# A gelu behind the next pair's copy, and a weight fold in rounded products among another block's matmuls

## The chip, the core and the metric

The kernel runs on one core of a Trainium2 chip. The core has TensorE (matmuls, called PE in the profile), VectorE (DVE), ScalarE (ACT), GpSimd (POOL) and SyncE (SP, which here only issues DMAs). The time is the device time of one execution in microseconds (us).

## What is computed

```python
x = A_x                                   # 2048 x 576
xn = _layernorm(x)
q, k, v = split(xn @ wqkv)                # 32 heads of 18
phi = lambda t: jnp.where(t > 0, t + 1, jnp.exp(t)) + 1e-6
kv = einsum("bhsd,bhse->bhde", phi(k), v) # one 18 x 18 state per head
z = einsum("bhsd->bhd", phi(k))           # sums over all tokens
o = (phi(q) @ kv) / (phi(q) . z + 1e-6)
s = o @ wo
g = silu(gelu(xn @ w1 + b1) @ w2 + b2)    # 576 -> 4608 -> 576
out = x + s * g
```

## The kernel before

All values are float32 and the error must stay small, so a matmul operand is split into a rounded part (`_h`, type fp32r) and the rest (`_l`, again fp32r), and a product is the sum of three rounded matmuls: h times h, h times l, l times h. To split, ScalarE casts (`split_w`, `set_hi`) and VectorE subtracts (`set_lo`). Some small matmuls are left in plain float32.

**First stage** (tiles `t` of 128 tokens, loop at L526): layernorm, projection to k and v (`project`, L310), phi(k), and the state, which is summed over all tiles in two PSUM banks (`state`, L379). A column of ones beside v (`VB`) gives the sums z as row 126 of the same banks.

**Between the stages** (L628 to L1079): the state of the last tile is summed, its blocks on the diagonal are copied into `kvz` with a mask, and z into `sums_k` (L635). Because the state doesn't depend on the token any more, `o @ wo` is rearranged: `fold_wo` (L681) multiplies the state with `wo` once, group by group (seven heads, 126 rows, to a group; the groups are `GROUPS`), into `kw`, and `attend` (L766) later multiplies each block's normalised phi(q) with `kw`. The fold makes 12 products of 288 columns in plain float32, each into one of two PSUM buffers (`bank1`); those of the left half (`h` = 0) are copied out by ScalarE, those of the right half by VectorE. `kw` is then moved by DMAs into tiles of 128 rows and split (`split_kw`). Two matmuls with the one-hot `last_row` spread z over all 128 rows (`zb_ps`), and ScalarE copies it to `zb`.

**Second stage** (loop at L1056, `i` from 1): for each block of 128 tokens `query` (L500; the name `pq`), `phi_query` (three ScalarE steps and one on VectorE), `by_sums` (GpSimd: phi(q) times z), `normalize` (VectorE: reduce, add, reciprocal; GpSimd: the product `pbuf`), `pad` (ScalarE copies 64 columns), `transpose_p` (TensorE, name `ptp`) and, three iterations later, `attend`.

**Third stage** (loop at L1502): the feed-forward net, in 18 steps: nine chunks of 512 hidden columns for the first half of the tokens and nine for the second. A chunk is two pairs of 256 hidden columns, `Up` (L1117), and then the products with W2 (`product`, L1266, name `pm`). Products of two by two blocks are made in seven matmul groups in place of eight, with sums and differences of operands, so `Up.step` runs seven groups of seven matmuls in the order 1, 2, 6, 5, 7, 3, 4: A, B, A, E, A, E, C. A and E are written more than once in the same PSUM bank: before group 6 adds into A, ScalarE must have copied group 1's value (`m1_sb`, L1152), before group 7 adds again it must have copied group 6's (L1158), and before group 3 adds into E it must have copied group 5's (L1162). Group 4's value C gets a VectorE sum (L1170) and then a gelu on ScalarE (L1171, the activation at L1143).

In the first half the weights are prepared beside this: GpSimd makes sums of W1 and W2, ScalarE and VectorE split them, and DMAs store them for the second half. A planner calls these pieces after fixed steps of a chunk (28 a chunk: 0 to 6 behind the first pair's groups, 7 to 13 behind the second's, then 14 of products): `PW2` for the splits of W2 (`hi` at the step, `lo` one step later), `PH` for the operands made of h (`S` sums on GpSimd, `hi` and `lo` splits). All engines but SP execute in the order in which the code is written (`in_order`), and SP's queue too is in order, so what stands ahead in an engine's queue holds all that is behind it.

Of the kernel before, what the change touches and what calls it, by code (L numbers as in the profile page):

```python
# [8 lines left out]
F32 = mybir.dt.float32  # L9
# [25 lines left out]
NSTG = 6  # L35
# [9 lines left out]
def linear_attention_gated_ffn(ctx, tc, x, xT, wqkv, wo, w1, w1e, b1, w2, b2, out):  # L45
# [68 lines left out]
    x_dram = dram.tile([P, 28, 512], F32, name="x_dram")  # L114

# [14 lines left out]
    zb = wqp.tile([P, D], F32, name="zb")  # L130


    ph1 = ExitStack()
    wkvp = ph1.enter_context(tc.tile_pool(name="wkvp", bufs=1, reuse_waits="tile"))
    stw = ph1.enter_context(tc.tile_pool(name="stw", bufs=2, reuse_waits="tile"))
    w2p = ph1.enter_context(tc.tile_pool(name="w2p", bufs=2, reuse_waits="tile"))
# [6 lines left out]
    last_row = t1.tile([P, P], F32, name="last_row", bufs=1)  # L143
    sums_k = t1.tile([P, D], F32, name="sums_k", bufs=1)
# [10 lines left out]
    def make_mask():  # L155

        nc.gpsimd.memset(sums_k, 0.0)
        nc.gpsimd.memset(last_row, 0.0)
        nc.gpsimd.affine_select(
            out=last_row, in_=last_row, compare_op=ALU.not_equal, fill=1.0, base=-G,  # L160
            pattern=[[0, P]], channel_multiplier=1,
        )
# [362 lines left out]
    raw_q = {}  # L525
    for t in range(NT):  # L526
# [101 lines left out]
    nc.sync.dma_start(b1c, b1)  # L628
    query(0)
    state(*pend)  # L630
    ln = GROUPS[-1][1]
    nc.vector.copy_predicated(kvz[:G, : 4 * G], mask[:G, :], ps_kv[0][:G, : 4 * G])
    nc.vector.copy_predicated(kvz[:ln, 4 * G : D], mask[:ln, :ln], ps_kv[1][:ln, :ln])
    nc.vector.copy_predicated(kvz[:ln, D:], mask[:ln, 8:ln], ps_kv[1][:ln, 8:ln])
    nc.scalar.copy(sums_k[96 : G + 1, : 4 * G], ps_kv[0][96 : G + 1, : 4 * G])  # L635
    nc.scalar.copy(sums_k[96 : G + 1, 4 * G :], ps_kv[1][96 : G + 1, :ln])
    query(1)
    zb_ps = bank2("zb_ps")
    for h in range(2):
        nc.tensor.matmul(  # L640
            zb_ps[:, h, :HD], last_row[: G + 1], sums_k[: G + 1, h * HD : (h + 1) * HD],
            start=True, stop=True,
        )
    ph1.close()
# [18 lines left out]
    ph2 = ExitStack()  # L663
    kwp = ph2.enter_context(tc.tile_pool(name="kwp", bufs=1, reuse_waits="tile"))
    t2 = ph2.enter_context(tc.tile_pool(name="t2", bufs=2, side="right", reuse_waits="tile"))
    wo_sb = []
    for i, (g, n) in enumerate(GROUPS):
        wo_sb.append(stage(D, f"wo{i}"))
        nc.sync.dma_start(wo_sb[i][:n], wo[g : g + n, :])
# [11 lines left out]
    def fold_wo():  # L681
# [7 lines left out]
        for i, n, at in [(i, G, i * G) for i in range(4)] + [(4, 8, 4 * G), (4, P, 512)]:  # L689
            rows = GROUPS[i][1]  # L690
            for h in range(2):
                hs = slice(h * HD, (h + 1) * HD)
                ps = bank1(f"ps_kw{i}{n}{h}")[:n, :HD]
                nc.tensor.matmul(  # L694
                    ps, kvz[:rows, at : at + n], wo_sb[i][:rows, hs], start=True, stop=True
                )
                if n < P:
                    if h:
                        nc.vector.tensor_copy(kw[i][:n, hs], ps)
# [15 lines left out]
            yield  # L715
# [340 lines left out]
    for i in range(1, NT + 4):  # L1056
        if 1 < i < NT:
            query(i)
# [3 lines left out]
        if i == 1:  # L1062
            phi_query(0)
            nc.scalar.copy(as2(zb), zb_ps[:, :, :HD])
            by_sums(0)
            groups, made = fold_wo(), []
            next(groups)
            steps = phi_steps(t2, pq.pop(1), "q1", made)
            next(steps)
            next(groups)  # L1070
            next(steps)
            next(groups)
            next(steps, None)
            phi_q[1] = made
            next(groups), next(groups)
            normalize(0)
            for _ in groups:
                pass
            pad(0)  # L1079
# [37 lines left out]
    class Up:  # L1117

# [26 lines left out]

        def step(self, i):
# [3 lines left out]
            if i == 1:  # L1150
                self.mm(A, 1)
                nc.scalar.copy(m1_sb, A)  # L1152
            elif i == 2:
# [14 lines left out]
            elif i == 4:  # L1168
                self.mm(C, 4)
                tt(C, C, u2_sb, op=ADD)  # L1170
                self.gelu(0, 1, C)  # L1171
# [279 lines left out]
    def plan_w1(add, w, base, T, hi, lo):  # L1451
# [16 lines left out]
    PW2 = {2: 0, 1: 1, 7: 3, 4: 6, 6: 7, 3: 9}  # L1468
    W2_NEXT = {1: 15, 2: 17, 7: 19, 4: 21, 5: 23, 3: 25, 6: 27}
    PH = dict(  # L1470
        S={(7, 0): 7, (5, 0): 8, (6, 0): 11, (3, 0): 11, (7, 1): 13, (5, 1): 14, (6, 1): 15, (3, 1): 15},
# [175 lines left out]
```

## Time and profile before

| | us |
|---|---|
| median of three runs (1110.47 to 1110.54) | 1110.5 |
| the profiled execution | 1110.38 |
| its span, first to last instruction | 1108.7 |
| TensorE busy | 1092.9 |
| VectorE busy | 788.5 |
| ScalarE busy | 545.5 |
| GpSimd busy | 453.1 |

In the rows shown below a timeline row gives the start, the time from the first start to the last end of the instructions merged in the row, the engine, the line, the operation with output and inputs, the shape and the count; the bracket at its end gives the idle time of the engine before it and what ended that. In the waits a row gives who waited for whom, the sum in us, the number of times and the longest. `a`, `bc` and `e` are the PSUM tiles of A, of B and C, and of E; `mid` holds the three copies, `g` the outputs of gelu.

### The profile page before, as it was taken

Reading aid. Unit: us, or ns where it says so; the run is one execution under the profiler, and the core shown is the slowest. Engines: PE = TensorE matmul, PEld = TensorE weight load, DVE = VectorE, ACT = ScalarE, POOL = GpSimd, SP = SyncE. Lnnn points to the kernel's source line nnn. Section 1 sums busy time; section 2 is a strip of 40 time slices with the busy share of each in tenths; the row PEclk is TensorE's granted clock in tenths of the full one; section 3 lists DMA queues with packets and bytes.
Section 4 is the critical chain, followed back from the end, with each engine's and each line's share of the span. In section 5 each row is a group of like instructions: output and inputs, shape, how many; then the busy total and the mean of one; then the engine's idle time right before and its main releaser. Section 6 shows DMA issues by size and latency. Waiting matters only on the chain.

```text
span 1108.7 us, 18087 instructions
## 1 busy us (share of the span) xinstructions
PE 1092.9 (99%) x6702; PEld 1007.6 (91%) x6702; DVE 788.5 (71%) x1096; ACT 545.5 (49%) x952; POOL 453.1 (41%) x394
## 2 busy tenths in 40 slices
PE   9999999999999999999999999999999999999998
PEld 8999989999898988989889889798898998989988
DVE  7766448888688887888878888565474564754756
ACT  6454555464646456464564645525244243353452
POOL 3555314332546445464454644325233233241340
PEclk9999999999999999999999999999999999999999
DMA  7997534675958559486584859977767667766452
GB/s 235 238 235 211 191 116 157 209 246 185 348 197 310 210 189 325 159 307 218 184 326 160 303 183 391 385 267 271 222 221 228 215 225 226 233 218 208 141 187 86
DMA packets 86960, 253.99 MB, mean 229 GB/s; under 512 B 11734, under 2 KB 24022, under 8 KB 84184
## 3 DMA queue, kind: packets, MB, share of 16 engines
q1 hardware_dynamic: 86872, 252.83, 68.0%
q8 instruction: 53, 0.87, 0.3%
q14 instruction: 35, 0.29, 0.1%
HBM read 156.27 MB, written 94.58 MB: 226 GB/s over the span
## 4 chain that ended last, share of the span: by engine, by line
PE 91%; DVE 3%; ACT 2%; issue 2%; DMA 2%; POOL 0%; SPq 0%; DVEq 0%; ACTq 0%; POOLq 0%
PE pm L1279 35%; PE a L1135 13%; PE e L1135 8%; PE bc L1135 8%; PE pk L321 6%; PE pq L321 5%; PE ps_s L775 5%; PE pv L321 4%; PE pd L1395 2%; DMA op<-w 2%; PE ps_kva L382 1%; PE ptp L757 1%; PE ps_kw L694 1%; DVE e L1174 1%; DVE bc L1170 1%
## 5 line engine op out<-in xcount | busy, mean ns | idle before, releaser
L1285 DVE TENSOR_TENSOR macc<-pm,macc 128x576 f32<-128x576 f32 x218 | 164.2, 753 | 53.5 <-PE pm L1279 52.4
L799 ACT CAST h_h<-g 128x512 fp32r<-128x512 f32 x204 | 122.6, 620 | 135.5 <-PE pm L1279 135.0
L802 DVE TENSOR_TENSOR h_l<-g,h_h 128x512 fp32r<-128x512 f32 x204 | 157.8, 777 | 15.7 <-ACT h_h L799 15.3
L1245 POOL TENSOR_TENSOR mid<-g 128x512 f32<-128x512 f32 x34 | 43.8, 1288 | 127.3 <-ACT g L1143 127.3
L1152 ACT COPY mid<-a 128x512 f32<-128x512 f32 x36 | 21.1, 587 | 95.2 <-PE a L1135 93.9
L1239 POOL TENSOR_TENSOR g<-g 128x512 f32<-128x512 f32 x34 | 52.2, 1536 | 35.8 <-ACT h_h L799 28.9
L1165 DVE TENSOR_TENSOR z<-a,mid 128x512 f32<-128x512 f32 x36 | 25.1, 698 | 51.8 <-PE a L1135 47.7
L845 POOL TENSOR_TENSOR w1raw<-w1raw 128x256 f32<-128x256 f32 x18 | 13.3, 738 | 116.8 <-ACT h_h L799 68.2
L1143 ACT ACTIVATE g<-bc,b1c 128x512 f32<-128x512 f32 x72 | 49.8, 691 | 18.1 <-DVE bc L1170 18.0
L1242 POOL TENSOR_TENSOR g<-g 128x512 f32<-128x512 f32 x34 | 52.6, 1547 | 10.7 <-DVE h_l L802 8.6
L1367 POOL TENSOR_TENSOR fin1l<-fin1h,fin1l 128x288 f32<-128x288 f32 x8 | 6.5, 808 | 120.9 <-DMA fin1l<-s_dram 73.0
L1155 DVE TENSOR_TENSOR bc<-bc,mid 128x512 f32<-128x512 f32 x36 | 25.0, 694 | 41.6 <-PE bc L1135 40.2
L1236 POOL TENSOR_TENSOR g<-g 128x512 f32<-128x512 f32 x34 | 47.6, 1399 | 2.7
L1158 ACT COPY mid<-a 128x512 f32<-128x512 f32 x36 | 21.1, 585 | 54.7 <-PE a L1135 54.7
L740 POOL TENSOR_TENSOR pbuf<-phiq,den 128x576 f32<-128x576 f32 x16 | 19.4, 1212 | 63.6 <-DVE den L739 63.6
L1166 ACT COPY mid<-a 128x512 f32<-128x512 f32 x36 | 21.1, 587 | 41.0 <-DVE z L1165 41.0
L321 PE MATMUL pk<-wkv_h,xh 128*128 128x288 f32 (+1 forms) x160 | 38.2, 321 | 0.5 <-DVE xh L251 0.5
L321 PE MATMUL pk<-wkv_l,xh 128*128 128x288 f32 (+1 forms) x160 | 38.2, 321 | 0.0
L775 PE MATMUL ps_s<-kw_h,th 128*128 128x288 f32 x160 | 35.5, 303 | 0.0
L802 DVE TENSOR_TENSOR h_l<-mid,h_h 128x512 fp32r<-128x512 f32 x34 | 34.1, 1004 | 1.9 <-ACT h_h L799 1.9
L1135 PE MATMUL a<-s,w 128*128 128x512 f32 x108 | 28.6, 400 | 6.4 <-ACT mid L1152 6.4
L321 PE MATMUL pq<-wq_h,xh 128*128 128x288 f32 x160 | 34.8, 299 | 0.0
(881 smaller groups left out, 3679.2 us busy)
## 6 DMA issues: line engine op xcount, KB each, us to landing
we<-we_dram SPq DMA_DIRECT2D x36, 448.0 KB
w2raw<-w SPq DMA_DIRECT2D x10, 1152.0 KB
w1raw<-w SPq DMA_DIRECT2D x18, 512.0 KB
op_a<-wa SPq DMA_DIRECT2D x18, 512.0 KB
op_c<-wc SPq DMA_DIRECT2D x18, 512.0 KB
op_d<-wd SPq DMA_DIRECT2D x18, 512.0 KB
wc<-op_c SPq DMA_DIRECT2D x18, 512.0 KB
wa<-op_a SPq DMA_DIRECT2D x18, 512.0 KB
```

The lines of the kernel that those rows point to most:

```text
L321: nc.tensor.matmul(ps[:, h, : ws.stop - ws.start], st, w[:, k, ws], start=(begin and i == 0), stop=(end and i == len(seq) - 1), skip_group ...
L775: nc.tensor.matmul(ps[:, h, :HD], st[:, k, :], w[:, k, h * HD : (h + 1) * HD], start=(i == 0), stop=(i == len(seq) - 1),)
L799: nc.scalar.copy(pair[0], src)
L802: eng.tensor_tensor(pair[1], src, pair[0].bitcast(F32), op=SUB)
L1135: nc.tensor.matmul(ps, st, mv, start=first and n == 0, stop=n == len(seq) - 1, skip_group_check=True,)
L1143: nc.scalar.activation(g, ps, AF.Gelu_apprx_tanh, bias=b1c[:, f : f + 1])
L1236: tt(src[5, pr], A(1, 0), A(1, 1), op=ADD)
L1239: tt(src[6, pr], src[5, pr], A(0, 0), op=SUB)
L1242: tt(src[3, pr], A(0, 1), src[6, pr], op=SUB)
L1245: tt(src[7, pr], A(0, 0), A(1, 0), op=SUB)
L1279: nc.tensor.matmul(ps[:, q, :HD], hs[p][st][:, cs], m[:, p, :], start=(n == 0 and i not in CHAIN), stop=(n == 5), skip_group_check=True,)
L1285: nc.vector.tensor_tensor(dst, src, dst, op=ADD)
```

## The change

It has five parts.

**The gelu of C** of the first pair of each chunk (even pair number `p`) isn't issued at the end of its pair, but in step 1 of the next pair, behind that step's copy of A. That of the second pair is issued where it was.

**Two entries of `PW2`**: W2's operand 4 is split at step 7 instead of 6, operand 6 at 8 instead of 7. **Two entries of `PH`'s sums**: (6, 1) at step 17 instead of 15, (3, 1) at 18 instead of 15.

**The fold** is made of rounded products: `wo` is split by ScalarE and VectorE behind the first query, and `kvz` behind its masked copies, and each of the 12 products becomes three rounded matmuls. The fold's generator now yields after each product. The third query is no longer made as a whole behind the fold: its 14 parts (two matmuls each) are written alternately with the products, one product behind each part from the third on. The three steps of the second query's phi are called at parts 4, 6 and 8, and the first query's `normalize` at part 10; a product's copy is written behind the part that follows it.

**z** isn't spread by matmuls any more: row 126 of `sums_k` (now the same memory as `zb`) is stored to DRAM and loaded back onto all rows. **`wo`** is loaded behind tile 14's work instead of behind the second query, and the pool `stg` has seven buffers instead of six. The pools of the first stage are closed in two steps, so that buffers of the third stage can hold the split `wo`.

```diff
-NSTG = 6
+NSTG = 7
...
+        if t == NT - 2:
+            for i, (g, n) in enumerate(GROUPS):
+                wo_sb.append(stage(D, f"wo{i}"))
+                nc.sync.dma_start(wo_sb[i][:n], wo[g : g + n, :])
...
     query(0)
+    for i in range(5):
+        split_wo(i)
+    for i in range(3):
+        wo_lo(i)
     state(*pend)
...
-    query(1)
-    zb_ps = bank2("zb_ps")
-    for h in range(2):
-        nc.tensor.matmul(
-            zb_ps[:, h, :HD], last_row[: G + 1], sums_k[: G + 1, h * HD : (h + 1) * HD],
-            start=True, stop=True,
-        )
+    nc.sync.dma_start(z_dram, sums_k[G : G + 1])
+    nc.sync.dma_start(
+        zb, bass.AP(tensor=z_dram.tensor, offset=z_dram.offset, ap=[[0, P], [1, D]])
+    )
...
+    nc.scalar.copy(kv_h[:G], kvz[:G])
+    for i in range(3, 5):
+        wo_lo(i)
+    nc.vector.tensor_tensor(kv_l[:G], kvz[:G], kv_h[:G].bitcast(F32), op=SUB)
+    query(1)
...
-                nc.tensor.matmul(
-                    ps, kvz[:rows, at : at + n], wo_sb[i][:rows, hs], start=True, stop=True
-                )
+                w = slice(at, at + n)
+                for k, (st, mv) in enumerate(((kv_h, 0), (kv_h, 1), (kv_l, 0))):
+                    nc.tensor.matmul(
+                        ps, st[:rows, w], wo_sb[i][mv][:rows, hs], start=k == 0, stop=k == 2
+                    )
+                yield
...
             phi_query(0)
-            nc.scalar.copy(as2(zb), zb_ps[:, :, :HD])
             by_sums(0)
             groups, made = fold_wo(), []
...
+            for k in range(n):
+                project(
+                    2, wq_h, wq_l, pq[2], PARTS[k : k + 1], begin=k == 0, end=k == n - 1
+                )
+                if k in (4, 6, 8):
+                    if k == 4:
+                        steps = phi_steps(t2, pq.pop(1), "q1", made)
+                    next(steps, None)
+                if k == 10:
+                    normalize(0)
+                if k > 1:
+                    next(groups)
...
+        def last(self):
+            C, f = self.bc[:, 1, :], 2 * self.p
+            self.g[0, 1] = g = gg.tile([P, 512], F32, tag="g", name="g")
+
+            def run():
+                nc.scalar.activation(g, C, AF.Gelu_apprx_tanh, bias=b1c[:, f : f + 1])
+
+            if self.p % 2:
+                run()
+            else:
+                Up.late.append(run)
...
                 nc.scalar.copy(m1_sb, A)
+                for late in Up.late:
+                    late()
+                Up.late.clear()
...
                 tt(C, C, u2_sb, op=ADD)
-                self.gelu(0, 1, C)
+                self.last()
...
-    PW2 = {2: 0, 1: 1, 7: 3, 4: 6, 6: 7, 3: 9}
+    PW2 = {2: 0, 1: 1, 7: 3, 4: 7, 6: 8, 3: 9}
```

How the rows stand on the engines: ScalarE in the second chunk of the first half, at the border of its two pairs (`bc2` and `e2` are the first pair's, `a3` the second's; `w2_1_` are splits of W2, `h10` of h). Before:

```order
L1143 ACTIVATE g_3884<-e2_3784,b1c_78 128x512
L1143 ACTIVATE g_3897<-bc2_3785,b1c_78 128x512
L799 CAST w2_1__3899<-w2raw1_3680 128x576
L1152 COPY mid_3293<-a3_3901 128x512
L799 CAST w2_1__3916<-w2raw1_3680 128x576
L799 CAST h10_h_3921<-g_3830 128x512
L1158 COPY mid_3293<-a3_3901 128x512
```

and now:

```order
L1176 ACTIVATE g_3921<-e2_3821,b1c_78 128x512
L1197 COPY mid_3330<-a3_3935 128x512
L1184 ACTIVATE g_3934<-bc2_3822,b1c_78 128x512
L828 CAST w2_1__3948<-w2raw1_3717 128x576
L828 CAST h10_h_3953<-g_3867 128x512
L828 CAST w2_1__3967<-w2raw1_3717 128x576
L1206 COPY mid_3330<-a3_3935 128x512
```

The first copy of A has moved ahead of the gelu of C and of one cast of W2; the same three casts stand between it and the next copy of A, and the gelu beside them.

GpSimd's rows stand in the same order before and now: the sums (6, 1) and (3, 1) follow the sum (5, 1) of the same pair and precede the next chunk's sums of weights, with nothing of GpSimd's written between the old and the new steps.

VectorE around the fold (`kw01` to `kw4` are the copies of the products' right halves, `phiq1` is phi of the second query, `den0` belongs to the first query's `normalize`). Before:

```order
L699 COPY kw01_1728<-ps_kw11261_1742 126x288
L699 COPY kw23_1729<-ps_kw21261_1753 126x288
L340 SCALAR_TENSOR_TENSOR phiq1_1761<-pq1_1648,eq1_1737 128x576
L699 COPY kw23_1729<-ps_kw31261_1766 126x288
L699 COPY kw4_1730<-ps_kw481_1776 8x288
L735 TENSOR_REDUCE den0_1780<-eq0_1720 128x32
L738 TENSOR_SCALAR den0_1780<-den0_1780 128x32
L739 RECIPROCAL den0_1780<-den0_1780 128x32
```

and now:

```order
L729 COPY kw01_1748<-ps_kw11261_1774 126x288
L334 SCALAR_TENSOR_TENSOR phiq1_1800<-pq1_1694,eq1_1764 128x576
L729 COPY kw23_1749<-ps_kw21261_1793 126x288
L764 TENSOR_REDUCE den0_1820<-eq0_1734 128x32
L767 TENSOR_SCALAR den0_1820<-den0_1820 128x32
L768 RECIPROCAL den0_1820<-den0_1820 128x32
L729 COPY kw23_1749<-ps_kw31261_1814 126x288
L729 COPY kw4_1750<-ps_kw481_1837 8x288
```

The copy of the sixth product (number 5, counted from 0) now stands behind phi of the second query, and that of the eighth (number 7) behind the first query's reduce, add and reciprocal.

More of the change, by code (lines that the diff above doesn't have):

```diff
@@ L114, in linear_attention_gated_ffn @@
     x_dram = dram.tile([P, 28, 512], F32, name="x_dram")
+    z_dram = dram.tile([1, D], F32, name="z_dram")
     rr_dram = dram.tile([2, P, 512], F32, name="rr_dram")
@@ L130, in linear_attention_gated_ffn @@
     zb = wqp.tile([P, D], F32, name="zb")
[L133 to L136, printed above, removed]
+    sums_k = zb
+    ph1, ph1w = ExitStack(), ExitStack()
+    wkvp = ph1w.enter_context(tc.tile_pool(name="wkvp", bufs=1, reuse_waits="tile"))
+    stw = ph1w.enter_context(tc.tile_pool(name="stw", bufs=2, reuse_waits="tile"))
+    w2p = ph1w.enter_context(tc.tile_pool(name="w2p", bufs=2, reuse_waits="tile"))
     t1 = ph1.enter_context(tc.tile_pool(name="t1", bufs=2, side="right", reuse_waits="tile"))
@@ L141, in linear_attention_gated_ffn @@
     nc.gpsimd.memset(tiny, 1e-6)
-    last_row = t1.tile([P, P], F32, name="last_row", bufs=1)
-    sums_k = t1.tile([P, D], F32, name="sums_k", bufs=1)
     v_bufs = [t1.tile([P, NG, P], F32, name=f"vb{i}", bufs=1) for i in range(2)]
@@ L155, in make_mask @@
     def make_mask():
[L157 to L161, printed above, removed]
-        )
         nc.gpsimd.memset(mf, 1.0)
@@ L627, in linear_attention_gated_ffn @@
         pend = (t, k_t, v_t)
[L628 to L636, printed above, removed]
-    query(1)
-    zb_ps = bank2("zb_ps")
-    for h in range(2):
-        nc.tensor.matmul(
-            zb_ps[:, h, :HD], last_row[: G + 1], sums_k[: G + 1, h * HD : (h + 1) * HD],
-            start=True, stop=True,
-        )
-    ph1.close()
+    ph1w.close()
     w1r = ctx.enter_context(tc.tile_pool(name="w1r", bufs=2, reuse_waits="tile"))
@@ L1117, in linear_attention_gated_ffn @@
     class Up:
+        late = []
         def __init__(self, n, w, xs):
```

56 lines of the change are left out of this document (38 added, 18 removed).

## The prediction

> **What bounds the kernel now.** I read the page first (busy time of each engine), then the waits of TensorE, then the timeline at the waits and at the place where the fold stands.
>
> ```profile
> PE 1092.9 (99%) x6702; PEld 1007.6 (91%) x6702; DVE 788.5 (71%) x1096; ACT 545.5 (49%) x952; POOL 453.1 (41%) x394
> ```
>
> ```profile
> PE a L1135 <- ACT mid L1152: 6.4, 9, 0.8
> ```
>
> The first line is the page's, the second the longest of TensorE's waits (us in total, times, longest). TensorE is busy for 1092.9 of 1108.7 us, so only two things shorten this kernel: matmul time taken away, or a wait of TensorE taken away. Busy time hides short waits, since the ends of matmuls are modelled; so I measure by the starts of matmuls. The waits name one repeated place: nine times TensorE waits before writing `a` a second time until ScalarE's copy of `a` (L1152) is done. Here is one of the nine, in the second of a chunk's two pairs (the first half of the program has nine chunks): B starts, then A again, then E, then A, then E.
>
> ```profile
> 387.41 0.39 PE L1135 MATMUL bc<-xh,wa 128*128 128x512 f32 x1
> ...
> 389.93 1.65 PE L1135 MATMUL a<-s,w 128*128 128x512 f32 x6 [0.76 <-ACT mid L1152]
> ...
> 391.65 1.53 PE L1135 MATMUL e<-s,wd 128*128 128x512 f32 x6
> ...
> 394.83 1.54 PE L1135 MATMUL e<-s,wc 128*128 128x512 f32 x6
> ```
>
> The same two blocks in a chunk of the second half, where nothing waits, and in the very first chunk:
>
> ```profile
> 755.93 0.39 PE L1135 MATMUL bc<-h0r,wa 128*128 128x512 f32 x1
> ...
> 759.10 1.07 PE L1135 MATMUL e<-s1r,wd 128*128 128x512 f32 x4
> ```
>
> ```profile
> 295.78 0.39 PE L1135 MATMUL bc<-xh,wa 128*128 128x512 f32 x1
> ...
> 299.58 0.62 PE L1135 MATMUL e<-s,wd 128*128 128x512 f32 x2
> ```
>
> B plus A take 3.17 us undisturbed (755.93 to 759.10), 4.24 where they wait (387.41 to 391.65) and 3.80 in the first chunk. The wait therefore costs 1.07 us eight times and 0.63 once, more than the 0.76 shown as idle, because the matmul pipeline is refilled behind it.
>
> **The gelu behind the copy.** ScalarE's row of work at that place:
>
> ```profile
> 388.14 0.69 ACT L1143 ACTIVATE g<-bc,b1c 128x512 f32<-128x512 f32 x1 [0.51 <-DVE bc L1170]
> 388.72 0.66 ACT L799 CAST w__4386<-w2raw 128x576 fp32r<-128x576 f32 x1
> 389.28 0.59 ACT L1152 COPY mid<-a 128x512 f32<-128x512 f32 x1
> ...
> 390.33 0.63 ACT L799 CAST h_h<-g 128x512 fp32r<-128x512 f32 x1
> ...
> 391.85 0.59 ACT L1158 COPY mid<-a 128x512 f32<-128x512 f32 x1 [0.88 <-PE a L1135]
> ...
> 394.00 0.60 ACT L1162 COPY mid<-e 128x512 f32<-128x512 f32 x1
> ```
>
> ```profile
> 387.42 0.68 DVE L1170 TENSOR_TENSOR bc<-bc,mid 128x512 f32<-128x512 f32 x1
> ```
>
> The copy of `a` stands behind the previous pair's last gelu, which waits for VectorE's sum (387.42 to 388.10), and behind a cast of W2. Its input was complete when B began (387.41) plus some 0.2 us. With the copy first it runs from about 387.6 to 388.2, and A can start when B ends, at 387.41 + 1.59 = 389.00 instead of 389.93.
>
> What the copy jumped stays on time: the gelu still waits for the same sum and starts at 388.14, and the cast of W2 follows at 388.72. So GpSimd's difference of h, which waits for that gelu, starts when it did. Next are the cast of h (389.28, 0.63) and the next cast of W2 (389.91, 0.66), done at 390.57. The next copy of `a` (L1158) now becomes due at about 390.8: it began 1.92 behind its A block, of which 0.13 was refill. It is therefore not held. From that copy to the copy of `e` (L1162) the queue is unchanged and takes 2.15 us (391.85 to 394.00), so the copy of `e` runs from 392.95 to 393.55. The E block that overwrites its source comes 3.18 behind the E before it (391.65 to 394.83), at 389.00 + 1.59 + 3.18 = 393.77. It came at 394.83 with the copy done at 394.60: the margin was 0.23 and stays 0.22. Late next is this copy, but just not late enough. I count no new wait there: the gain is 8 x 1.07 + 0.63 = 9.2 us, and I take 9.0, because a margin of 0.2 will not hold in every chunk. The bounds are 9.2 and, if the margin is missed by 0.5 in each of nine chunks, 4.5.
>
> In the second half's nine chunks the gelu is also moved behind the copy, and there TensorE did not wait before; there are no casts of W1 and W2 there, so I count nothing.
>
> **The two sums on GpSimd** are written two and three steps later, but GpSimd executes its instructions in written order, and in that order they have the same neighbours before and after: nothing moves, 0 us. The stores of two W2 operands go past one load of `we` on SP's queue; TensorE reads that load a chunk later, so this too is 0.
>
> **The fold.** TensorE's rows: the two `zb` matmuls, the fold, the third query, its transposes; then the transposes of the third block.
>
> ```profile
> 153.18 1.13 PE L640 MATMUL zb_ps<-sums_k,last_row 127*128 127x288 f32 x4
> 154.15 7.53 PE L694 MATMUL ps_kw<-wo,kvz 126*126 126x288 f32 x24
> 161.30 0.64 PE L321 MATMUL pq<-wq_h,xh 128*128 128x288 f32 x2
> ...
> 162.04 0.43 PE L321 MATMUL pq<-wq_h,xl 128*128 128x288 f32 x2
> ...
> 165.24 0.71 PE L757 MATMUL ptp<-ident,pbuf 128*128 128x128 f32 x5
> ...
> 174.00 0.71 PE L757 MATMUL ptp<-ident,pbuf 128*128 128x128 f32 x5
> ```
>
> From 162.04 to 165.24 stand twelve pairs of rounded matmuls of 288 columns: 0.267 a pair, 0.133 each. The new stretch from 153.18 on holds 14 such pairs (3.73) and 12 products of three (36 x 0.133 = 4.80): 8.53 us, where 12.06 stood (153.18 to 165.24). If nothing waited, TensorE would be at the transposes 3.5 us sooner, at 161.7. It will wait, for three reasons, each from these rows:
>
> ```profile
> 157.66 0.78 ACT L338 ACTIVATE eq<-eq,tiny 128x576 f32<-128x576 f32 x1
> ...
> 158.47 0.76 DVE L340 SCALAR_TENSOR_TENSOR phiq<-pq,eq 128x576 f32<-128x576 f32 x1
> ...
> 160.43 0.45 DVE L699 COPY kw<-ps_kw 8x288 f32<-8x288 f32 x1 [0.74 <-PE ps_kw L694]
> 160.80 0.73 DVE L735 TENSOR_REDUCE den<-eq 128x32 f32<-128x576 f32 x1
> ...
> 162.28 1.17 POOL L740 TENSOR_TENSOR pbuf<-phiq,den 128x576 f32<-128x576 f32 x1 [5.75 <-DVE den L739]
> 163.40 1.43 POOL L727 TENSOR_TENSOR eq<-phiq,zb 128x576 f32<-128x576 f32 x1
> 164.87 0.75 DVE L735 TENSOR_REDUCE den<-eq 128x32 f32<-128x576 f32 x1 [2.06 <-POOL eq L727]
> 166.31 1.55 POOL L740 TENSOR_TENSOR pbuf<-phiq,den 128x576 f32<-128x576 f32 x1 [1.47 <-DVE den L739]
> 166.76 1.72 DVE L364 TENSOR_TENSOR kw_l<-kr,kw_h 128x576 fp32r<-128x576 f32 x1
> 168.40 0.74 DVE L340 SCALAR_TENSOR_TENSOR phiq<-pq,eq 128x576 f32<-128x576 f32 x1
> ...
> 173.77 0.24 ACT L749 COPY pbuf<-pbuf 128x64 f32<-128x64 f32 x1 [1.29 <-POOL pbuf L740]
> ```
>
> First, the products have two PSUM buffers, so product j waits until product j-2 has been copied out; by the pitch of 0.667 product j ends at 154.38 + 0.667 j. ScalarE copies the even products in time. VectorE's copy of product 5 now stands behind phi of the second query, whose ScalarE step comes behind the copy of product 4 (157.25), so that phi ends at about 159.1, as before; the copy ends near 159.55, and product 7, due at 158.65, loses 1.0. VectorE's copy of product 7 stands behind the first query's reduce, add and reciprocal (160.80 to 162.13, 1.33), which now begin at 159.5: product 9 loses another 0.35. TensorE reaches the transposes at about 163.1 and, with ScalarE's padding behind its last two casts, ends them 1.6 sooner than before.
>
> Second, behind that reduce stands a chain that had no slack: den, GpSimd's `pbuf` (162.28) and `eq` (163.40), the second reduce (164.87), two splits, phi (168.40), and so on to the padding at 173.77, on which the last of the transposes at 174.00 waits. It sets when the third block's transposes run, whatever TensorE gains ahead of it. The first reduce comes 1.3 sooner (159.5 for 160.80); the second is held until about 164.05 by VectorE's work on the last two products (0.82 sooner than 164.87); from there the chain is the same, row for row. So 0.85 us sooner at 174.00 is what is left of 3.5. In this chain one split takes 1.72 (166.76) beside GpSimd's product at 166.31; I leave it in, since both move together. The Trainium skill ("SBUF — State Buffer", section "Who interferes with whom") says that a VectorE instruction with two SBUF inputs and a GpSimd instruction that reads SBUF exclude each other for a whole instruction. The trace agrees: the split ends 0.62 behind the end of that product. By that rule, if they no longer met, the chain would be about 1.0 us shorter and the fold would bring some 1.9.
>
> Third, `zb` now comes through DRAM in two DMAs instead of two matmuls and a copy.
>
> ```profile
> 150.73 0.21 ACT L636 COPY sums_k<-ps_kvb 31x72 f32<-31x72 f32 x1
> ...
> 155.12 1.41 POOL L727 TENSOR_TENSOR eq<-phiq,zb 128x576 f32<-128x576 f32 x1 [4.71 <-ACT zb L1064]
> ```
>
> ```profile
> 182.70 0.33 SPq L932 DMA_DIRECT2D rr_dram<-wa_rest0q  x1
> 184.71 0.32 SPq L937 DMA_DIRECT2D wa_rest0ef<-rr_dram  x1
> ```
>
> The sums are ready at 150.94 as before. A store of 256 KB had landed 2.0 us after its issue (182.70, when the load that needs it went out at 184.71); two such transfers give 155.1, when GpSimd's product started before anyway. It is needed by 157.9 (159.5 less 1.41 and hand-over). SP waits in that time, but what is queued behind it, the moves of the fold's rows, isn't ready before 157.
>
> ```profile
> 140.00:160.00 20.00, 19.94 (x119) 16.21 (x117) 6.50 (x12) 10.86 (x22) 1.96 (x7) 1.00 0.35 109
> ```
>
> The splits of wo and of the state (six casts on ScalarE, six subtractions on VectorE, 0.6 to 0.7 each by the casts above) are laid over time that both engines have: in this slice of 20 us (busy PE, PEld, DVE, ACT, POOL, then the clock, the share of the DMA engines and GB/s) VectorE works 6.50 and ScalarE 10.86. The last of them, the state's cast and subtraction, stand behind the sums (150.94) and end some 1.5 later, at 152.5; the first product is due at 153.98. wo is loaded a tile sooner, and the DMA engines are 0.35 busy. Cost: nothing, with 1.5 us to spare; if this cover were gone, each us past 153.98 would cost one. So the fold gives 0.85: bounds 0 (the chain or a late `zb` takes all) and 3.5; the value is near the chain's end, since its rows follow on each other without a gap.
>
> **Sum.** The profiled execution took 1110.38 us (span 1108.7 and 1.7 around it), 0.1 under the median of the runs. 1110.4 - 9.0 - 0.9 = 1100.5.
>
> **The rivals.** (1) A new wait in place of the old: the margin of 0.22 at the copy of `e` is missed by about 0.5 in each of nine chunks. For it: one more operation stands between the two copies of `a` than before, and 0.2 is little. Against: the queue from there on moves as a whole. 9.0 becomes 4.5: 1105.0. (2) The fold brings all 3.5, because the chain is shortened where splits and products no longer meet: 1097.9. For it: the split of 1.72, over twice the cast of the same 576 columns (0.66). Against it: that is 1.0 at most, and the rest of the chain is the order of the program. (3) Slower: `zb` late. GpSimd waits for it, behind it VectorE's reduce, behind that the copy of product 7, and so TensorE. Each us past 157.9 costs one.
>
> ```profile
> 35.41 1.58 POOL L282 TENSOR_TENSOR xt<-xt,bc 128x640 f32<-128x640 f32 x1 [6.38 <-DMA bc<-st_dram]
> ```
>
> For it: such a broadcast from DRAM kept GpSimd waiting 6.4 us here. It decides from 167.8 on, when 9.9 us of gain are used up, that is with over 8 us for each transfer; at 9.0 each the time is 1111.6. Against it: that wait is from the loading stage, and here the DMA engines are 0.35 busy. (4) That the change doesn't do what it says holds for the two sums alone and costs nothing.
>
> **Numbers.** My forecast 0.77 (own range 1099 to 1102), rival 1 0.13, rival 2 0.08, rival 3 0.02. The range 1098.0 to 1104.0 takes in rival 2 and the better part of rival 1. About 0.2%, 2.2 us, is what a measurement of this kernel can tell from no change: faster 0.96, same 0.02, slower 0.02.
>
> **What would show it.** Right: the waits of TensorE no longer list L1152's copy; B plus A take 3.2 in every chunk of the first half; the third block's transposes start near 173.1, with a wait on VectorE's copies in the fold. Wrong: a list headed by the copy of `e` or the second copy of `a`, or transposes at 170.5, or GpSimd waiting for a DMA at 155.

## The result and the profile after

The changed kernel takes 1100.4 us (1100.1 to 1100.5) against 1110.5 (1110.47 to 1110.54) before, measured on one chip: ratio 0.9908, 95% interval 0.9891 to 0.9926. Its profiled execution took 1100.49 us (span 1098.8). The prediction was 1100.5.

The waits of TensorE in the changed kernel (us in total, times, longest; rows of 0.4 and more, without a wait of 2.0 at the very start that both kernels have). Line numbers have moved: the copy of `a` that headed the list before is L1197 now, the second copy of `a` L1206, the copy of `e` L1210.

```profile
PE e L1168 <- ACT mid L1210: 0.9, 2, 0.6
PE ptp L786 <- DVE phiq L334: 0.6, 1, 0.6
PE ps_kw L723 <- DVE kw L729: 0.5, 1, 0.5
PE ps_kw L723 <- ACT kw L731: 0.5, 2, 0.2
PE pk L315 <- ACT xh L242: 0.4, 1, 0.4
PE a L1168 <- ACT mid L1206: 0.4, 1, 0.4
```

L1197 isn't listed at all. The waits on L1210 and L1206 are not new: the kernel before has the same two rows with the same numbers; they lie in the first pair of each half's first chunk, not where the change works. The two rows on `ps_kw` and the one on `phiq` are new; all lie in and behind the fold.

Where the 9.9 us of span came from is read from four starts of TensorE: the first query, the beginning of the third stage, the first chunk of its second half, and its last chunk; first before, then after.

```profile
144.60 0.43 PE L321 MATMUL pq<-wq_h,xh 128*128 128x288 f32 x2
...
282.48 0.39 PE L1135 MATMUL a<-xh,wa 128*128 128x512 f32 x1
...
703.91 0.50 PE L1135 MATMUL a<-h1r,wc 128*128 128x512 f32 x1 [0.41 <-ACT mid L1158]
...
1076.39 0.39 PE L1135 MATMUL bc<-h1r,wd 128*128 128x512 f32 x1
```

```profile
144.79 0.43 PE L315 MATMUL pq<-wq_h,xh 128*128 128x288 f32 x2
...
281.70 0.39 PE L1168 MATMUL a<-xh,wa 128*128 128x512 f32 x1
...
694.02 0.50 PE L1168 MATMUL a<-h1r,wc 128*128 128x512 f32 x1 [0.41 <-ACT mid L1206]
...
1066.48 0.39 PE L1168 MATMUL bc<-h1r,wd 128*128 128x512 f32 x1
```

Up to the first query 0.19 is lost. The traces differ by 0.1 at the first projection already; in the ten kernels here with the new fold this query starts anywhere from 144.40 to 144.82, whatever was changed behind it, and in the three with the old fold from 144.23 to 144.60. I take the 0.19 for chance; a real loss of 0.1 or 0.2 is not excluded. From there to the third stage 136.91 us where 137.88 stood: 0.97 gained, by the fold. Through the first half of the third stage 412.32 where 421.43 stood: 9.11, by the gelu. Through the second half 372.46 where 372.48 stood: nothing. These stretches repeat: the fold's is 137.87 to 137.88 in the three kernels with the old fold and 136.91 to 136.93 in the four with the changed one, and the first half takes 412.32 in `gelu_alone` below too.

The pair of a chunk that the prediction showed, in the changed kernel, first TensorE's rows, then ScalarE's:

```profile
384.95 0.39 PE L1168 MATMUL bc<-xh,wa 128*128 128x512 f32 x1
...
386.54 1.52 PE L1168 MATMUL a<-s,w 128*128 128x512 f32 x6
...
388.12 1.52 PE L1168 MATMUL e<-s,wd 128*128 128x512 f32 x6
...
391.30 0.39 PE L1168 MATMUL e<-s,wc 128*128 128x512 f32 x1
```

```profile
385.21 0.59 ACT L1197 COPY mid<-a 128x512 f32<-128x512 f32 x1
385.69 0.70 ACT L1184 ACTIVATE g<-bc,b1c 128x512 f32<-128x512 f32 x1
386.27 0.68 ACT L828 CAST w__4435<-w2raw 128x576 fp32r<-128x576 f32 x1
...
388.32 0.59 ACT L1206 COPY mid<-a 128x512 f32<-128x512 f32 x1 [0.29 <-PE a L1168]
...
390.47 0.60 ACT L1210 COPY mid<-e 128x512 f32<-128x512 f32 x1
```

B plus A take 3.17 (384.95 to 388.12). Counted from B's start, gelu, cast, second copy and copy of `e` stand at 0.74, 1.32, 3.37 and 5.52; the prediction put them at 0.73, 1.31, 3.4 and 5.54. The copy of `e` is done at 391.07, 0.23 ahead of the E block at 391.30.

In the fold, VectorE's and GpSimd's rows that answer to those shown of before:

```profile
159.01 0.76 DVE L334 SCALAR_TENSOR_TENSOR phiq<-pq,eq 128x576 f32<-128x576 f32 x1 [1.32 <-ACT eq L332]
159.69 0.45 DVE L729 COPY kw<-ps_kw 126x288 f32<-126x288 f32 x1
160.05 0.74 DVE L764 TENSOR_REDUCE den<-eq 128x32 f32<-128x576 f32 x1
...
164.50 0.74 DVE L764 TENSOR_REDUCE den<-eq 128x32 f32<-128x576 f32 x1
```

```profile
155.97 1.41 POOL L756 TENSOR_TENSOR eq<-phiq,zb 128x576 f32<-128x576 f32 x1 [19.51 <-DVE kw L729]
```

The last row puts GpSimd's wait down to a VectorE copy that the product doesn't read. Its phi was done at 154.87, so what it waited for is `zb`; in the trace of `sums_first` below the same wait is put down to the DMA of `zb`.

### The profile page after: what moved, and what is told of

Its sections match the earlier page's. It is cut to its first block, busy times and chain, and to the rows that moved or that the text cites. A ratio compares the mean times of both kernels' runs of the same rounds, so it can differ in the third digit from the quotient of the medians.

```text
span 1098.8 us, 18128 instructions
## 1 busy us (share of the span) xinstructions
PE 1087.3 (99%) x6710; PEld 1008.3 (92%) x6710; DVE 805.3 (73%) x1102; ACT 548.5 (50%) x957; POOL 457.1 (42%) x391
## 4 chain that ended last, share of the span: by engine, by line
PE 96%; DVE 1%; ACT 1%; DMA 1%; SPq 0%; issue 0%; POOL 0%; ACTq 0%; DVEq 0%; POOLq 0%
PE pm L1327 35%; PE a L1168 15%; PE e L1168 10%; PE bc L1168 10%; PE pk L315 6%; PE ps_s L804 5%; PE pq L315 5%; PE pv L315 4%; PE pd L1443 2%; PE ps_kva L376 1%; PE ptp L786 1%; PE warm L363 0%; DMA b2b<-b 0%; DVE macc L1343 0%; PE ps_kvb L376 0%
## 5 line engine op out<-in xcount | busy, mean ns | idle before, releaser
L831 DVE TENSOR_TENSOR h_l<-g,h_h 128x512 fp32r<-128x512 f32 x204 | 162.9, 802 | 14.9 <-ACT h_h L828 13.9
L1197 ACT COPY mid<-a 128x512 f32<-128x512 f32 x36 | 21.1, 587 | 110.8 <-PE a L1168 110.6
L1287 POOL TENSOR_TENSOR g<-g 128x512 f32<-128x512 f32 x34 | 52.2, 1536 | 20.8 <-ACT h_h L828 18.9
L1290 POOL TENSOR_TENSOR g<-g 128x512 f32<-128x512 f32 x34 | 52.6, 1546 | 7.6 <-DVE h_l L831 5.5
L1284 POOL TENSOR_TENSOR g<-g 128x512 f32<-128x512 f32 x34 | 50.2, 1477 | 2.7
L1206 ACT COPY mid<-a 128x512 f32<-128x512 f32 x36 | 21.1, 587 | 44.1 <-PE a L1168 44.1
L831 DVE TENSOR_TENSOR h_l<-mid,h_h 128x512 fp32r<-128x512 f32 x34 | 38.1, 1120 | 2.2 <-ACT h_h L828 2.2
L756 POOL TENSOR_TENSOR eq<-phiq,zb 128x576 f32<-128x576 f32 x16 | 22.8, 1428 | 29.0 <-DVE kw L729 19.5
L315 PE MATMUL pq<-wq_l,xh 128*128 128x288 f32 x160 | 34.3, 296 | 0.0
```

Source lines behind the costliest of these rows:

```text
L315: nc.tensor.matmul(ps[:, h, : ws.stop - ws.start], st, w[:, k, ws], start=(begin and i == 0), stop=(end and i == len(seq) - 1), skip_group ...
L831: eng.tensor_tensor(pair[1], src, pair[0].bitcast(F32), op=SUB)
L1284: tt(src[5, pr], A(1, 0), A(1, 1), op=ADD)
L1287: tt(src[6, pr], src[5, pr], A(0, 0), op=SUB)
L1290: tt(src[3, pr], A(0, 1), src[6, pr], op=SUB)
```

## The experiments

In what follows "the third block's transposes" are timed from the start of the first query, so that the chance of the first stage drops out: 29.40 before (174.00 less 144.60), 28.83 after:

```profile
173.62 0.71 PE L786 MATMUL ptp<-ident,pbuf 128*128 128x128 f32 x5
```

Single runs of one kernel spread by 0.3 to 1.4 us. Steps of less than 1 us between kernels are therefore read from such stretches of the traces, not from the medians alone.

### The gelu and the casts of W2 apart

The kernel before with one of the two each:

```diff
+                for late in Up.late:      # gelu_alone, with last() as in the change
+                    late()
```
```diff
-    PW2 = {2: 0, 1: 1, 7: 3, 4: 6, 6: 7, 3: 9}      # w2_alone
+    PW2 = {2: 0, 1: 1, 7: 3, 4: 7, 6: 8, 3: 9}
```

> The kernel before with the gelu of C moved behind the copy of a, and nothing else (the two casts of W2 keep steps 6 and 7, so the first of them stands ahead of the copy). Theory: that cast has its operand early and runs in ScalarE's free time ahead of the copy (1.6 us free there), so the copy starts when its matmuls are done and the whole of 9.1 us comes: 1101.4. Rival: the cast isn't ready early or delays the copy by its 0.66 in eight chunks, and about half the gain is lost: 1105 to 1106.

Measured 1101.4 (ratio 0.9917, 0.9903 to 0.9930). ScalarE's rows:

```profile
385.15 0.69 ACT L1144 ACTIVATE g<-e,b1c 128x512 f32<-128x512 f32 x1 [1.61 <-DVE e L1190]
385.73 0.66 ACT L799 CAST w__4385<-w2raw 128x576 fp32r<-128x576 f32 x1
386.29 0.59 ACT L1165 COPY mid<-a 128x512 f32<-128x512 f32 x1
```

The cast, still ahead of the copy, follows the other gelu at once, in time in which ScalarE had waited. The copy ends at 386.88, and the A block starts undisturbed at 387.21. The first half of the third stage takes 412.32, as in the changed kernel. The gelu alone carries the third stage's gain; moving the casts added nothing.

> The kernel before with only the two casts of W2 one step later, so that no cast stands between the gelu and the copy of a. Theory: the gelu still waits for VectorE's sum and ends at about 388.7 in the chunk shown; the copy follows it directly, 0.56 sooner than before, so each of eight chunks gains about 0.56 (none in the first chunk, where no cast stood there): 1106.0, with a wait on that copy of some 0.2 to 0.3 left. Rival: the place of the casts is of no account and only the gelu counts: 1110.5.

Measured 1105.2 (0.9951, 0.9937 to 0.9965). The wait on the copy, now, and the cast in the first chunk, before:

```profile
PE a L1135 <- ACT mid L1152: 1.5, 8, 0.2
```

```profile
296.65 0.67 ACT L799 CAST w__3410<-w2raw 128x576 fp32r<-128x576 f32 x1
```

B plus A take 3.66 where 4.24 stood: 0.58 in eight chunks. Most of the 0.8 by which the time is below the expected 1106.0 is the first chunk, where B plus A take 3.23 for 3.80: a cast stood between gelu and copy there too, and the expectation said that none did. So without the cast some half of the wait goes, without the gelu all of it: the gelu waits itself, and a cast behind it can't use the time ahead.

### The other parts

`fold_alone` is the changed kernel with gelu, casts and sums put back; `sums_undone` has only the two sums put back.

```diff
-        S={..., (6, 1): 17, (3, 1): 18},      # sums_undone
+        S={..., (6, 1): 15, (3, 1): 15},
```

> The changed kernel with the gelu, the casts of W2 and the two sums put back: only the fold in rounded products, z through DRAM and the earlier load of wo remain. Theory: the parts are independent; the third stage starts 0.8 sooner and keeps it: 1109.7. Rival 1: the fold's gain is absorbed later (0): 1110.5. Rival 2: more than 0.8 belongs to the fold, up to 1.5 since the trace of the changed kernel started its second stage 0.18 later: 1109.0.

> The changed kernel with the two sums of h on GpSimd written at step 15 again. Theory: GpSimd executes in written order and both have the same neighbours, so nothing moves: 1100.4. Rival: written earlier, they are released earlier and meet VectorE's splits of h in more chunks, 0.2 to 0.3 in each of nine: 1102 to 1103.

Measured 1109.5 (0.9990, 0.9981 to 0.9999) and 1100.5 (0.9909, 0.9895 to 0.9922). `fold_alone` gains 1.1 over the kernel before, timed beside it. The interval only just leaves out no change, but its trace repeats the changed kernel's fold (136.91); its list of waits is headed by the copy of `a` with 6.4 us, as before. The sums do nothing that can be seen. 9.2 of `gelu_alone` and 1.1 of `fold_alone` make 10.3, against 10.1 of all parts: within the noise they add up.

### How much room the copy of `e` has

```diff
                 nc.scalar.copy(u1_sb, A)
+                if self.twice:      # second pair of a chunk, first half
+                    nc.scalar.copy(u1_sb, A)
```

> The changed kernel, where in the second pair of each of the first half's nine chunks ScalarE makes the second copy of a (group 6's value) twice. Copies follow each other at 0.48, so the copy of e comes 0.48 later. Theory: its margin is 0.23, as the trace shows (390.47 + 0.60 against 391.30), so TensorE waits 0.25 and loses some 0.1 more for the refill, in nine chunks: 3.2 more, 1103.6, and the list of waits is headed by the copy of e. Rival 1: the margin in the trace isn't real and nothing was to spare: 0.6 in each chunk, 1105.8. Rival 2: more is to spare than the rows show, or the casts of W2 give way: 1100.4.

Measured 1106.1 (0.9960, 0.9946 to 0.9973), 5.7 more. The number is rival 1's, the mechanism the theory's. ScalarE's rows:

```profile
389.56 0.58 ACT L1207 COPY mid<-a 128x512 f32<-128x512 f32 x1 [0.29 <-PE a L1169]
390.18 0.59 ACT L1209 COPY mid<-a 128x512 f32<-128x512 f32 x1
...
392.32 0.60 ACT L1213 COPY mid<-e 128x512 f32<-128x512 f32 x1
```

The second copy into the same place starts 0.62 behind the first, not 0.48, so the copy of `e` comes 2.76 behind the first copy of `a` instead of 2.15. Of these 0.61 the margin takes 0.23; 0.38 remain, and the two blocks around it take 2.02 and 1.73 for 1.59 and 1.59: 0.57 in each of nine chunks, 5.1. The list of waits is headed by that copy, as the theory said (nine new waits and the two of before), and also has new waits of the products for casts of h, 0.5 in all:

```profile
PE e L1169 <- ACT mid L1213: 3.1, 11, 0.6
```

The margin is as small as the rows say.

### What limits the fold

`plain_fold` goes back to plain float32 products, in the new mixed order; `two_banks` writes the products in turn into two banks taken once.

```diff
-                for k, (st, mv) in enumerate(((kv_h, 0), (kv_h, 1), (kv_l, 0))):
-                    nc.tensor.matmul(
-                        ps, st[:rows, w], wo_sb[i][mv][:rows, hs], start=k == 0, stop=k == 2
-                    )
+                nc.tensor.matmul(      # plain_fold
+                    ps, kvz[:rows, w], wo_sb[i][2][:rows, hs], start=True, stop=True
+                )
```
```diff
+        pair = [bank1("ps_kwl"), bank1("ps_kwr")]      # two_banks
...
-                ps = bank1(f"ps_kw{i}{n}{h}")[:n, :HD]
+                ps = pair[h][:n, :HD]
```

> The changed kernel with the fold's 12 products in plain float32 again (one matmul in place of three, which the chip runs as two passes), still alternating with the third query's parts; the splits of wo and of the state are still made, but not used. Theory: a product takes 0.63 in place of 0.40, so the last of them ends at 164.6 in place of 163.5; the second reduce stands behind it by VectorE's last subtraction and comes 1.1 later, and so do the third block's transposes: 1101.5, that is, a unit worse than the kernel with the old fold. Rival 1: all 2.7 of matmul time count: 1103.1. Rival 2: the mixing, not the rounding, brought the gain, and the waits hide the longer products: 1100.4.

Measured 1100.85 (0.9913, 0.9900 to 0.9927): between the theory and rival 2, and not worse than the old fold (`gelu_alone`, 1101.4). Two products of it, among the third query's parts of 0.267:

```profile
154.71 0.65 PE L722 MATMUL ps_kw<-wo,kvz 126*126 126x288 f32 x2
155.46 0.65 PE L722 MATMUL ps_kw<-wo,kvz 126*126 126x288 f32 x2
```

A plain product costs 0.75 less 0.267, that is 0.48, against 0.40 rounded: the pitch of 0.63 that I had read from the old fold (7.53 for 12) was held by the copies out of its two buffers, not by the matmuls (the weight loads of the old fold wait ten times for these copies, 3.8 us in all). The third block's transposes come at 29.35, 0.52 later than with rounded products and 0.05 sooner than before. Up to there rounding brings 0.5, and mixing alone next to nothing. Behind them this kernel gains 0.4 as the changed one does: its third stage starts 137.44 behind the first query, where 137.88 and 136.91 stood.

> The changed kernel, where the fold's products are written strictly in turn into two PSUM banks taken once (left halves into one, right halves into the other), since in the trace the fourth and the eighth product wait 0.23 each for ScalarE's copy of the product just before them. Theory: those two were given their forerunner's bank. The fourth product then starts 0.38 sooner (156.16), the second query's phi and the first reduce come 0.38 sooner (159.67 for 160.05), the eighth product waits for VectorE's copy instead, and the third block's transposes run 0.4 sooner than 173.62: 1100.0. Rival: what is gained is lost again in the chain behind the second reduce (GpSimd's product meets the split of 1.72 in another way): 1100.4.

Measured 1100.1 (0.9906, 0.9893 to 0.9920); transposes at 28.36, 0.47 sooner, near the theory's 0.4. The changed kernel waits as follows:

```profile
156.54 0.53 PE L723 MATMUL ps_kw<-wo_w,kvh 126*126 126x288 f32 x2 [0.23 <-ACT kw L731]
...
159.69 0.40 PE L723 MATMUL ps_kw<-wo_h,kvh 126*126 126x288 f32 x1 [0.23 <-ACT kw L731]
...
161.76 0.29 PE L723 MATMUL ps_kw<-wo_h,kvh 72*8 72x288 f32 x1 [0.48 <-DVE kw L729]
```

The first two are the fourth and the eighth product, each waiting for ScalarE's copy of the product just before it, which a strict turn of two buffers would not ask for; with the two banks in turn the fourth starts 0.67 behind the third, and the eighth waits for VectorE's copy instead (0.71).

Then the order on VectorE and GpSimd, in `sums_first` and `copies_first`. Both also have the two banks, and the third group's right copy ahead of the second query's phi:

```diff
     def normalize(t):      # sums_first and copies_first
+        if t > 1:
+            by_sums(t)
         if t:
-            by_sums(t)
...
-                    next(steps, None)
+                    if k < 8:
+                        next(steps)
...
-            phi_q[1] = made
+                if k == 8:
+                    next(steps, None)
+                    phi_q[1] = made
+                    by_sums(1)
```
```diff
-                if k == 10:      # copies_first
-                    normalize(0)
                 if k > 1:
                     next(groups)
...
+                if k == 10:
+                    normalize(0)
```

> Two banks in turn as in two_banks, and the right half's copy of the third group written ahead of the second query's phi on VectorE, and GpSimd's product of the second query with z written ahead of the first query's pbuf. Theory: the chain of reduces and the copies limit the fold. The eighth product no longer waits; the tenth still does, behind the first reduce (by 0.8); the transposes of the first block begin at 162.8 for 163.49, the second reduce at 163.9 for 164.50, and the third block's transposes come 0.65 sooner: 1099.7. Rival 1: the second reduce was held by GpSimd's eq alone and now comes 1.5 sooner: 1098.9. Rival 2: ScalarE's queue (casts, padding, phi of the third query) sets the time and nothing moves: 1100.4.

Measured 1100.35 (0.9909, 0.9895 to 0.9922), transposes at 28.66: no better than `two_banks`. The number is rival 2's; the wait is the theory's, but 1.25 long instead of 0.8. The rows of GpSimd, VectorE and TensorE say why:

```profile
159.10 1.41 POOL L757 TENSOR_TENSOR eq<-phiq,zb 128x576 f32<-128x576 f32 x1 [2.07 <-DVE phiq L334]
```

```profile
158.93 0.74 DVE L766 TENSOR_REDUCE den<-eq 128x32 f32<-128x576 f32 x1
159.71 0.84 DVE L769 TENSOR_SCALAR den<-den 128x32 f32<-128x32 f32 x1
```

```profile
161.30 0.30 PE L724 MATMUL ps_kwr<-wo_h,kvh 72*8 72x288 f32 x1 [1.25 <-DVE kw L730]
```

The addition on 128x32, 0.18 elsewhere, lasts until GpSimd's product ends (160.55 and 160.51), and behind it stands the copy for which the tenth product waits.

> As sums_first, but the first query's reduce, addition and reciprocal are written behind VectorE's copy of the eighth product instead of ahead of it. Theory: the wait of 1.25 before the tenth product is what held the fold in sums_first; VectorE's copy now ends at about 159.6, the tenth product is on time at 159.9, the twelfth waits some 0.4 for the copy of the tenth behind the reciprocal, the first block's transposes begin at 162.1 for 163.06 and the second reduce at 163.1 for 164.06; the third block's transposes come 0.95 sooner than in sums_first: 1099.3. Rival 1: the chain goes by ScalarE's casts, padding and phi of the third query, which don't move: 1100.2. Rival 2: GpSimd's early product and VectorE's small instructions hold each other up and take back half of it: 1099.8.

Measured 1098.9 (1098.7 to 1099.1; 0.9894, 0.9880 to 0.9907): 1.4 below the changed kernel, whose fastest run took 1100.1. No product waits on a copy of `kw` any more in the list, and the transposes come at 27.40, 1.26 sooner than in `sums_first`, where the theory had 0.95:

```profile
160.02 0.29 PE L724 MATMUL ps_kwr<-wo_h,kvh 72*8 72x288 f32 x1
...
172.05 0.71 PE L788 MATMUL ptp<-ident,pbuf 128*128 128x128 f32 x5
```

> As copies_first, with the split of the second block of kw moved one block later, so that the subtraction that took 1.72 beside GpSimd's pbuf no longer stands ahead of the third query's phi on VectorE. Theory: that phi then waits for ScalarE alone and starts about 0.55 sooner, and so do the third block's transposes: 0.5 less than copies_first, 1098.8. Rival: it meets GpSimd's next product and holds the next block's chain in the same way, or TensorE has other work by then: as copies_first.

```diff
-        for k in {2: (0, 1), 3: (2,)}.get(i, ()):
+        for k in {2: (0,), 3: (1, 2)}.get(i, ()):      # split_later
```

Measured 1099.65 (0.9901, 0.9888 to 0.9915), 0.7 more than `copies_first`: the rival's mechanism, though it expected no loss. The second block's transposes come 0.64 sooner (22.05 for 22.69), but the moved split meets the next `pbuf`; the third block's come 0.22 later (27.62 for 27.40), and from the fourth block on all is 0.64 later:

```profile
169.14 2.33 DVE L358 TENSOR_TENSOR kw_l<-kr,kw_h 128x576 fp32r<-128x576 f32 x2
171.50 0.76 DVE L334 SCALAR_TENSOR_TENSOR phiq<-pq,eq 128x576 f32<-128x576 f32 x1
```

```profile
169.39 1.46 POOL L771 TENSOR_TENSOR pbuf<-phiq,den 128x576 f32<-128x576 f32 x1 [1.56 <-DVE den L770]
```

### z late

```diff
+    z_hops = [z_dram] + [dram.tile([1, D], F32, name=f"z_hop{i}") for i in range(3)]
     nc.sync.dma_start(z_dram, sums_k[G : G + 1])
+    for i in range(3):
+        nc.sync.dma_start(z_hops[i + 1], z_hops[i])
+    z_dram = z_hops[3]
```

> The changed kernel with z sent through three more rows of DRAM before it is loaded onto all rows, so that zb is late. Theory: it has 2.6 us to spare now (GpSimd's product with z ends at 157.4, the first reduce could not begin before 160.05), and each us behind that costs one: the reduce waits for it, behind the reduce VectorE's copy of the eighth product, and behind that TensorE. The one-row store took 1.2 from issue to the next issue; at 1.2 to 2.0 for each hop the product starts at 159.6 to 162.0 and the time is 1101.4 to 1103.8. Rival: the stalls that the fold has anyway take it in, and nothing is seen up to some 2 us of lateness: 1100.4 to 1101.4.

Measured 1104.4 (0.9944, 0.9931 to 0.9958), 4.0 more than the changed kernel and above the upper end. GpSimd's product, then TensorE behind it:

```profile
161.22 1.40 POOL L760 TENSOR_TENSOR eq<-phiq,zb 128x576 f32<-128x576 f32 x1 [25.15 <-DMA zb<-z_hop]
```

```profile
164.37 0.41 PE L727 MATMUL ps_kw<-wo_h,kvh 72*8 72x288 f32 x1 [3.95 <-DVE kw L733]
164.57 0.44 PE L727 MATMUL ps_kw<-wo_l,kvh 72*8 72x288 f32 x1
164.81 0.44 PE L727 MATMUL ps_kw<-wo_h,kvl 72*8 72x288 f32 x1
```

Against the start of the first query the product comes 5.64 later, 1.9 for each hop, and the first reduce 2.99 later. But the third block's transposes come 4.39 later, at 33.22. Behind the wait of 3.95 the matmuls follow each other at 0.24 instead of 0.133. The table by windows (length, busy PE, PEld, DVE, ACT, POOL, then the granted clock, the share of the DMA engines and GB/s):

```profile
156.00:160.00 4.00, 3.78 (x29) 3.41 (x28) 1.58 (x3) 2.16 (x5) 0.00 (x0) 1.00 0.22 66
160.00:164.00 4.00, 0.42 (x4) 0.18 (x2) 1.28 (x4) 0.39 (x1) 1.40 (x1) 0.77 0.50 157
164.00:168.00 4.00, 3.63 (x16) 3.40 (x17) 1.22 (x4) 0.71 (x3) 2.53 (x2) 0.50 0.26 77
```

This long wait cost twice: once itself, and once at a clock of 0.50.

## Why the prediction was right, point by point

**The measure and the bound** held. Starts of matmuls gave 9.2 us for the wait, and 9.11 came; the list's 6.4 would have been too little.

**The gelu.** Each row came where it was put, and `gelu_alone` shows that this is the cause. I took 9.0 for 9.2 because the margin of 0.2 would "not hold in every chunk". It held in all nine; `copy_twice` shows that it is real: a copy of `e` 0.6 later costs 5.7, so rival 1's mechanism exists, but nothing in the change set it off. The casts of W2, which the prediction lets pass behind the copy together with the gelu, had no need to: they fit ahead of it. **Second half, sums, the stores on SP's queue**: nothing, as said (the stores were not tried alone).

**The fold** came out at 0.97 where 0.85 stood, but not by the steps given, so that it came this near is luck. At the third block's transposes, where I had put all of it, 0.57 arrived. The step that failed is the working of the stalls. Counting products from 0, as the prediction does, I had product 7 lose 1.0, product 9 lose 0.35 and product 3 nothing. By the starts of matmuls products 3 and 7 (the fourth and the eighth above) lost 0.5 each and product 9 lost 0.6: 1.6 for 1.35, in other places. The two products that were given their forerunner's bank were not foreseen; the first of them pushed the second query's phi, and so the first reduce, to 160.05 (less the 0.19, 159.86 for 159.5). `two_banks` gives back 0.47. The other 0.4 was gained between those transposes and the third stage: the blocks of the second stage follow each other at 7.99 instead of 8.01 in every kernel with the new fold. `plain_fold` has it too, so it isn't the rounding. Why `attend`'s matmuls run that little closer is open; no experiment aimed at it.

**The chain without slack** was read rightly: from the second reduce to the third block's transposes it takes 9.12 (164.50 to 173.62) where 9.13 stood (164.87 to 174.00). But I took its start as given. In `copies_first` it starts sooner, and the transposes come at 27.40, where 28.83 stood in the changed kernel; the two banks account for 0.47 of that, the order on VectorE and GpSimd for the rest (no run tells the order on the one from that on the other). The third stage then starts 135.41 behind the first query: 2.5 of rival 2's 3.5, though not by rival 2's mechanism, since the split still takes 1.72 there. `split_later` moved that split, and it met GpSimd again a block later. That agrees with the rule of the Trainium skill that the prediction weighed. The addition in `sums_first` has only one SBUF input. The same section of the Trainium skill ("SBUF — State Buffer", "Who interferes with whom") says that `tensor_scalar` can enter a mode that takes the shared ports, while `tensor_reduce` never contends; the trace agrees with both: the addition took 0.84 for 0.18, and the reduce 0.74 beside the same product, as long as elsewhere.

**z.** The splits were done at 152.55 (152.74 less 0.19), where 152.5 stood. The product with z started at 155.97, not 155.1, and waited for the DMA. The prediction had named that a sign of being wrong; it cost nothing, since 2.6 us were left until the reduce. Rival 3's price, one for one, was too low: 2.99 cost 4.39, since the clock was lower behind the long wait. If those 1.4 are paid once (an estimate from this one run), the sign turns 1.4 sooner than at the 167.8 that I gave; no run went that far.

**The sum and the range.** 1100.4 against 1100.5 is in part luck: the gelu gave 0.1 more than its term and the later blocks 0.4 that no term held, while the chain gave 0.3 less and the profiled execution lost 0.2 ahead of the first query. The range is not what the prediction says of it: 1098.0 to 1104.0 leaves out rival 2's time (1097.9), and rival 1's (1105.0) too.

## What to carry over

An instruction that itself waits must not stand ahead of a copy that TensorE waits for, when its own readers have time: here its new place cost nobody anything, since all that it passed was ready earlier. Price such a wait by the starts of matmuls around it, since the refill behind it was nearly a third of it. Where a stretch of matmuls is shortened, write down first what the other engines' queues hold between its copies: their order, with the two banks taken in turn, brought 1.4 us here, the shorter products 0.5.

## What the hardware showed that I had not expected

After 3.95 us without a matmul the granted clock was 0.50 over the next four us (`z_hops`), and matmuls of 288 columns started 0.24 apart instead of 0.133; from 169.0 on they started 0.133 apart again. The Trainium skill ("TensorE: Matmul & The Clock Gate", "Part 1: The HAM clock gate (the "warmup" mystery)") says that the clock halves after an idle window of about 3.4 us and needs a busy one to return; this trace agrees.

A small VectorE addition (128x32, 0.18) took 0.84 beside a GpSimd product and ended 0.04 behind it (160.55 and 160.51); in `copies_first`, where it began later, it again ended 0.04 behind the product (160.69 and 160.65). On ScalarE a copy made again to the same place started 0.62 behind the first (`copy_twice`), where the next instruction starts 0.48 behind a copy (385.21 and 385.69 above); why is not shown. A plain float32 product of 288 columns cost 0.48 against 0.40 for its three rounded matmuls.
